# Half a group sooner: moved key sums, projections and key products in an attention kernel with a gated projection behind it

## The chip, the cores and the metric

The kernel runs on one core of one Trainium2 chip. Its metric is the device time of one execution in microseconds (us), the median of several. A second execution is recorded by the hardware profiler; its rows say when each instruction of each engine began and how long it took. The engines are TensorE (PE, with its weight loads as PEld), VectorE (DVE), ScalarE (ACT), GpSimd (POOL), and SyncE (SP), which only issues transfers.

## What is computed

```python
kv_pool = kv.reshape(B, H // 4, 4, W // 4, 4, C).mean(axis=(2, 4))
k = v = kv_pool.reshape(B, -1, C) @ w_sr          # 768 keys of 128 for each of 4 batches
s = (q @ k.transpose(0, 2, 1)) / sqrt(C)          # q: 4 x 12288 x 128
a = exp(s - s.max(-1));  a /= a.sum(-1) + 1e-9
x = a @ v
gate = sigmoid(causal depthwise convolution of x over 5 rows, weights conv_w)
out = (gate * (x @ w_val)) @ w_out
```

All inputs and the output are fp32.

## The kernel before

The 12288 queries of a batch are 24 groups of 512 (`GQ`), 96 groups in all (`G`), and a group is four steps of 128 queries (`NT`). One Python loop over steps `t` writes the order of all engines out by hand: the schedule is manual, so every engine runs its instructions in the order in which the lines of the loop issue them. `j` is the step within the current group; `gi, mj` are group and step lagging by one, and the work of older groups is hung on `mj`.

A step's own work: `score` (L381) makes 128 x 768 scores in PSUM in three passes (queries and keys in a high and a low part), always two steps' worth in the steps with odd `j`. There are three pairs of banks for them. `row_max` (L397, DVE), `expo` (L414, ACT), `norm` (L423, reciprocal of the sum on DVE, with the sum scaled by ACT where `scaled_by_act` says so, else by DVE), `p_hi` (L445, ACT: the fp16 high part `hl`) and `p_lo` (L448, DVE: the remainder, after which the bank is free for the score three steps on). `p_lo` of a group's last step issues the transposing transfer `turn` (L438, SP).

The older groups' work, before the change: the value products of group gi-2 (`av_slice`, L465, PE, in all four steps); x of group gi-3 is written by ACT at mj 0 (`g_x`, L476); the convolution runs on POOL for two groups at a time (`conv_step`, L498: five tap products L491 and four adds L496, spread over eight steps; the last add completes the gate at mj 2 of an odd gi); group gi-6 has its value projection at mj 2 (`g_val`, L549, two fp32 halves; `g_val_parts`, L544, three passes where `split_x`, L537, has made a high and a low part of x on POOL, one group in four), its tanh at mj 2 and the gated product h at mj 3 (`g_h`, L553, DVE); group gi-7 has its output projection at mj 0 (`g_out`, L560) and its evacuation at mj 1 (`g_evac`, L570, ACT). Projections and key products share one PSUM bank, `m` (`misc`, L59), so each has to wait for the user before it. ACT makes the high part of the queries of group gi+2 at mj 3 (`g_qh`, L353) and POOL the low part (`g_ql`, L358).

The next batch's keys are made meanwhile: `plan` (L293) gives places (group, step) to the sums over 4 x 4 pixels (`pool_kv`, L127, DVE), and from these the groups of key products (`setup_product`, L320, at mj 1), column maxima (`column_max`, L196), the scale (`column_scale`, L202), and the high and low parts of the keys (`keys_high`, L235, ACT; `keys_low`, L239, POOL). At each batch boundary `values_parts` (L274) splits the values on POOL in three groups. The last batch, from group 72 on, has no keys to prepare. Output is stored four groups at a time; `held` keeps a store back until the next four are ready, until `CATCH_UP`.

After the loop the last groups (n7 = 89 to n1 = 95) are finished by a list of calls (L820 to L887).

Of the kernel before, what the change touches and what calls it, by code (L numbers as in the profile page):

```python
# [27 lines left out]
def attn_moe_kernel(ctx, tc, qT, kvT, w_sr, w_moe, outT):  # L28
# [264 lines left out]
    def plan():  # L293

        for b in range(1, B):
            st, k0 = states[b], (b - 1) * NG
            if b == 1:
                places = [(k, j) for k in range(4, 21) for j in range(2)] + [(9, 2), (14, 2)]
                loads.update({1: (b, 5), 5: (b, 6), 13: (b, 7)})
                works = [(i, 0, PC) for i in range(WHOLE)]  # L300
            else:
                places = [(-3, 2)] + [(k, j) for k in range(-2, 21) for j in range(2)] + [(-2, 2)]
                early = (-7, -3, -1, 3, 5, 9, 11, 15)
                loads.update({k0 + k: (b, p) for p, k in enumerate(early)})
                works = []
# [7 lines left out]
            for q in range(4):  # L313
                last = max(p for p, w in zip(places, works) if w[0] < (q + 1) * PIECES // 4)
                k = k0 + last[0] + 1
                products[k], highs[k + 1] = (b, q), (b, q)
                maxima[k] = b, q
            scales[k0 + 22] = b
# [8 lines left out]
    def setup_vector(gi, j):  # L327
# [3 lines left out]
        if (gi, j) in sums:  # L331
            b, w = sums[gi, j]
            pool_kv(states[b], *w)
        if j == 2 and gi in maxima:
            b, q = maxima[gi]
            column_max(states[b], q)
        if gi in scales:
            st = states[scales[gi]]
            if j == 0:
                st["scale"] = column_scale(st)  # L340
            for _ in range((3, 2, 1)[j]):
                st["scale"].pop(0)()
# [68 lines left out]
    def scaled_by_act(g, j):  # L411
        return j == 1 or j > 1 and g.i < 9 - j

# [122 lines left out]

    def split_x(g):  # L537
        g.xh, g.xl = (work.tile([C, GQ], F32R, name=n, bufs=1) for n in ("xh", "xl"))
        x = g.x[:, HALO:HALO + GQ]
        nc.gpsimd.tensor_copy(out=g.xh, in_=x)  # L540
        return lambda: nc.gpsimd.tensor_tensor(out=g.xl, in0=x, in1=g.xh.bitcast(F32),
                                               op=ALU.subtract)

# [152 lines left out]
    evac = None  # L696
    held, CATCH_UP, low = [], (B - 1) * NG + 9, None
    for t in range(NT * G + LAG):
# [3 lines left out]
        gi, mj = divmod(t - LAG, NT)  # L702
        avg, xg, vg, og = (at(gi - d) for d in (2, 3, 6, 7))
        cg = at(gi - 4 - gi % 2)

        def projections(c0, c1):
            if og and mj == 0:
                g_out(og.h, og.m, c0, c1)
            if vg and mj == 2:
                if vg.xh is None:  # L710
                    g_val(vg, vg.m, c0, c1)
                elif c0 == 0:
                    g_val_parts(vg, vg.m)

        if og and mj == 0:
            og.m = misc()
        if vg and mj == 2:
            vg.m = misc()
# [15 lines left out]
        if xg and mj == 0:  # L734
            new_x(xg)
            g_x(xg, xg.av)
        if og and mj == 1:
            out_tile(og)
            g_evac(og, og.m)
        evac = None  # L740
        if vg and mj == 2:
            vg.th = g_tanh(vg.gate)
        if gi == 1 and mj > 0:
            evac = values(st, mj - 1)
        elif mj == 1 and gi > 0:
            evac = setup_product(gi)
        if avg:
            av_slice(avg, AV_CUTS[mj], AV_CUTS[mj + 1])
        if cg:
            if mj == 0 and cg.i == gi - 4:  # L750
                halo(cg, at(cg.i - 2), nc.gpsimd)
            conv_step(cg, gi % 2 * 4 + mj)
        if mj == 2 and gi > 7 and gi % 4 == 1:
            low = split_x(at(gi - 5))
        if mj == 3 and gi >= 0 and at(gi + 2):
            g_qh(at(gi + 2))
# [10 lines left out]
        if mj == 1 and gi in highs:  # L767
            b, q = highs[gi]
            keys_high(states[b], q)
        if vg and mj == 3:  # L770
            vg.h = g_h(vg.th, vg.m)
        if gi >= 0 and mj < 3:
            setup_vector(gi, mj)
        if mj == 1 and gi in loads:
            b, p = loads[gi]
# [6 lines left out]
        if mj == 3 and gi in highs:  # L782
            b, q = highs[gi]
            keys_low(states[b], q)
        if mj == 3 and low:
            low()
            low = None
        if mj == 3 and 0 < (gi + 2) // NG < B and (gi + 2) % NG < 3:
# [5 lines left out]
        if mj == 3 and gi >= 0 and at(gi + 2):  # L794
            g_ql(at(gi + 2))
        if og and mj == 2 and og.i % 4 == 3:
            held.append(og)
            if gi > CATCH_UP or len(held) > 1:
                store_last(held.pop(0), 4)
        if gi == CATCH_UP and mj == 2:  # L800
            store_last(held.pop(0), 4)
# [15 lines left out]
    def av_bank():  # L817
        return ps_av.tile([C, GQ], F32, name="av")

    new_x(n3)  # L820
    g_x(n3, n3.av)
    a0, a1 = two()
    n6.m, n5.m = g_val(n6, a0), g_val(n5, a1)
    av_slice(n2, 0, 18)
# [3 lines left out]
    conv_first(n4, acc4)  # L828
    n7.m = g_out(n7.h, misc())
    gate3 = conv_pool(n3)  # L830
# [7 lines left out]
    conv_first(n2, acc2)  # L838
    out_tile(n7)
    g_evac(n7, n7.m)  # L840
    store_last(n7, 2)
# [12 lines left out]
    g_x(n1, avs[0], 0, half)  # L854
    n4.m = g_val(n4, one())
    acc1 = one()
# [3 lines left out]
    n3.m = g_val(n3, av_bank())  # L860
    n4.h = g_h(n4.th, n4.m)
    g_x(n1, avs[1], half, GQ)
    conv_first(n1, acc1[:, half:], half, GQ)
    conv_rest(n1, acc1[:, half:], half, GQ)
# [51 lines left out]
```

## Time and profile before

| | us |
|---|---|
| median of 3 runs | 988.25 (988.19 to 988.72) |
| the profiled execution | 987.91 |
| its span in the trace | 986.1 |

Times of rows are from the span's start. A row of the chain of waits reads: start, length, engine, output tile, line, count. A row of the timeline reads: start, length, engine, line, operation, out<-in, shape, count, and in brackets the idle time ahead of it with what ended it. Matmuls overlap in a row of the timeline; in the chain their lengths add up. Stretches give busy time of each engine and, in brackets, its instructions.

### The profile page before, as it was taken

The numbers are of one execution on the slowest core, as the hardware profiler recorded it, in microseconds if no ns is written. First come the engines' busy times: TensorE is split into PE (matmuls) and PEld (weight loads), VectorE is DVE, ScalarE is ACT, GpSimd is POOL, SyncE is SP. The second block draws the span as 40 slices with busy tenths as digits, with TensorE's granted clock in tenths as the row PEclk, the third lists the DMA queues.
The fourth block names the chain that finished last, engine by engine and source line by source line (L and its number), as shares of the span: only waits on it lengthen the run. The fifth ranks groups of instructions, "written<-read, shape, count | busy, mean of one in ns | idle before, by whom it ended". The sixth has DMA issues, their size and how long they took to land.

```text
span 986.1 us, 14838 instructions
## 1 busy us (share of the span) xinstructions
PE 957.4 (97%) x4837; PEld 718.3 (73%) x4837; DVE 923.1 (94%) x1736; ACT 914.0 (93%) x1698; POOL 908.9 (92%) x700
## 2 busy tenths in 40 slices
PE   4699999999999999999999999999999999999998
PEld 3467777777777777777777777777777777777774
DVE  6999999999999999999999999999999999999996
ACT  2999999999999999999999999999999999999995
POOL 2769999999999999999999999999999999999993
PEclk9999999999999999999999999999999999999999
DMA  9999999999999999999999999999999999999996
GB/s 346 276 220 219 206 163 262 213 244 222 262 238 248 235 257 237 241 249 239 237 241 237 257 229 242 259 229 221 210 221 231 211 217 266 229 195 216 195 213 156
DMA packets 615070, 228.97 MB, mean 232 GB/s; under 512 B 599248, under 2 KB 600400, under 8 KB 609232
## 3 DMA queue, kind: packets, MB, share of 16 engines
q1 hardware_dynamic: 614992, 228.02, 108.4%
q8 instruction: 38, 0.62, 0.3%
q14 instruction: 40, 0.33, 0.1%
HBM read 50.66 MB, written 25.17 MB: 77 GB/s over the span
## 4 chain that ended last, share of the span: by engine, by line
PE 84%; DVE 6%; ACT 5%; POOL 4%; DMA 1%; issue 1%; SPq 0%; POOLq 0%; ACTq 0%; DVEq 0%
PE s L374 35%; PE av L462 33%; PE m L561 7%; PE m L550 6%; ACT hl L446 2%; DVE hl L450 2%; POOL acc L496 2%; ACT s L415 1%; PE m L546 1%; DVE nm L399 1%; DMA pt<-in_kv 1%; POOL tap L491 1%; POOL ql L361 1%; DVE pool L128 0%; DVE s L517 0%
## 5 line engine op out<-in xcount | busy, mean ns | idle before, releaser
L496 POOL TENSOR_TENSOR acc<-acc,tap 128x1024 f32<-128x1024 f32 x184 | 437.0, 2375 | 7.2
L462 PE MATMUL av<-pt,vv 128*128 128x512 f16 x1728 | 404.3, 378 | 0.0
L450 DVE SCALAR_TENSOR_TENSOR hl<-s,r,hl 128x768 f16<-128x768 f32 x384 | 388.4, 1011 | 12.6 <-ACT hl L446 9.0
L399 DVE TENSOR_REDUCE nm<-s 128x1 f32<-128x768 f32 x382 | 361.6, 947 | 17.1 <-PE s L374 6.5
L446 ACT ACTIVATE hl<-s,r 128x768 f16<-128x768 f32 x384 | 346.0, 901 | 16.2 <-DVE r L431 5.0
L415 ACT ACTIVATE s<-s,nm 128x768 f32<-128x768 f32 x384 | 335.7, 874 | 20.3 <-DVE nm L399 14.3
L462 PEld LDWEIGHTS <-vv 128*128 128x128 f16 x1746 | 167.8, 98 | 184.6 <-issue 6.1
L374 PE MATMUL s<-kh,qh 128*128 128x384 f32 x764 | 260.2, 422 | 10.1 <-DVE hl L450 8.3
L491 POOL TENSOR_SCALAR tap<-x,wm 128x1024 f32<-128x1024 f32 x184 | 203.9, 1121 | 0.0
L374 PE MATMUL s<-kh,ql 128*128 128x384 f32 x764 | 195.9, 338 | 0.1
L374 PE MATMUL s<-kl,qh 128*128 128x384 f32 x764 | 195.4, 337 | 0.0
L374 PEld LDWEIGHTS s<-kh,qh 128*128 128x128 f32 x764 | 143.0, 190 | 53.6 <-PE s L374 9.0
L361 POOL TENSOR_TENSOR ql<-q,qh 128x512 fp32r<-128x512 f32 (+1 forms) x97 | 123.2, 1271 | 17.8 <-ACT qh L356 17.8
L374 PEld LDWEIGHTS s<-kh,ql 128*128 128x128 f32 x764 | 138.1, 189 | 0.8 <-POOL ql L361 0.4
L374 PEld LDWEIGHTS s<-kl,qh 128*128 128x128 f32 x764 | 138.5, 188 | 0.0
L561 PE MATMUL m<-h,wm 128*128 128x256 f32 x358 | 106.6, 379 | 0.0
L550 PE MATMUL m<-x,wm 128*128 128x256 f32 x274 | 81.5, 379 | 0.0
L431 DVE RECIPROCAL r<-z 128x1 f32<-128x1 f32 x384 | 61.8, 161 | 10.3
L477 ACT ACTIVATE x<-av,down 128x512 f32<-128x512 f32 x96 | 65.3, 680 | 5.0 <-PE av L462 5.0
L491 POOL TENSOR_SCALAR acc<-x,wm 128x1024 f32<-128x1024 f32 x46 | 51.5, 1120 | 14.8 <-ACT x L477 11.6
L561 PEld LDWEIGHTS m<-h,wm 128*128 128x128 f32 x358 | 64.5, 188 | 0.2
L556 DVE SCALAR_TENSOR_TENSOR h<-th,m 128x512 f32<-128x512 f32 x90 | 60.9, 677 | 0.0
(124 smaller groups left out, 654.9 us busy)
## 6 DMA issues: line engine op xcount, KB each, us to landing
q<-in_q SPq DMA_DIRECT2D x23, 1024.0 KB, 6.0
out<-o SPq DMA_DIRECT2D x22, 1024.0 KB, 4.8
kvt<-in_kv SPq DMA_DIRECT2D x21, 768.0 KB, 5.3
pt<-in_kv SPq DMA_DIRECT2D x12, 384.0 KB, 6.7
o<-in_kv SPq DMA_DIRECT2D x3, 768.0 KB, 9.5
pt<-hl SPq DMA_TRANSPOSE x98, 10.3
out<-o SPq DMA_DIRECT2D x3, 512.0 KB, 2.7
kvt<-in_kv SPq DMA_DIRECT2D x2, 384.0 KB, 7.3
```

Source lines behind the costliest of these rows:

```text
L361: nc.gpsimd.tensor_tensor(out=g.ql[:, c0:c1], in0=g.q[:, c0:c1], in1=g.qh[:, c0:c1].bitcast(F32), op=ALU.subtract)
L374: nc.tensor.matmul(g.s[j][:, h], a[:, sl], k[:, h * HALF:(h + 1) * HALF], start=(i == 0), stop=(i == 2))
L399: nc.vector.tensor_reduce(out=nm, in_=g.s[j], axis=AX.XY, op=ALU.max, negate=True)
L415: nc.scalar.activation(out=g.s[j], in_=g.s[j], func=AF.Exp, bias=g.nm.pop(j), accum_out=g.z[j])
L446: nc.scalar.activation(out=part(g, j, 0), in_=g.s[j], func=AF.Copy, scale=g.r[j])
L450: nc.vector.scalar_tensor_tensor(out=part(g, j, 1), in0=g.s.pop(j), scalar=g.r.pop(j), in1=part(g, j, 0), op0=ALU.mult, op1=ALU.subtract)
L462: nc.tensor.matmul(out, g.st["vv"][:, v, k], g.pt[:, j0:j1, a * NCH + k], start=(i == 0), stop=(i == len(AV_ORDER) - 1))
L477: nc.scalar.activation(out=g.x[:, HALO + c0:HALO + c1], in_=av, func=AF.Copy, scale=g.st["down"])
L491: nc.gpsimd.tensor_scalar(out=t, in0=g.two[:, k:k + 2 * GQ], scalar1=cwt[:, k:k + 1], scalar2=1.0, op0=ALU.mult, op1=ALU.mult)
L496: nc.gpsimd.tensor_tensor(out=g.acc, in0=g.acc, in1=t, op=ALU.add)
L550: nc.tensor.matmul(m[:, c0:c1], wval, g.x[:, HALO + c0:HALO + c1], start=True, stop=True)
L561: nc.tensor.matmul(m[:, c0:c1], wout, h[:, c0:c1], start=True, stop=True)
```

## The change

- The key sums go to steps 0 and 3 in place of 0 and 1; the places (-3, 2) and (-2, 2) of batches 2 and 3 become (5, 2) and (12, 2). The key products are issued at mj 3, the column maxima a group later at step 0, the operations of the scale at steps 1, 2 and 3.
- The value projection of group gi-6 moves to mj 0, tanh and h to mj 1, the output projection (now of the same group gi-6) to mj 2, its evacuation to mj 3. `CATCH_UP` becomes group 79 and the stores follow at mj 3. The high part of the queries moves to mj 2.
- POOL's two operations that split x stand together at mj 0 of every fourth group, ahead of that group's two adds, and no longer at mj 2 and 3 behind them.
- In the last batch (`QUIET`) one more group in four is projected in parts: ACT writes xh at mj 1, DVE xl at mj 2 (groups 70, 74, 78, 82, 86, 90); for groups 91 and 92 ACT writes xh and POOL xl, in the tiles of the queries.
- `scaled_by_act` changes: steps 0 and 2 of groups 1 to 5 besides step 1 of all groups.
- Behind the loop, n7 is finished but for its store; n6, n5 and n4 are projected in parts; h of n4 is made by POOL (two operations) and ACT (a copy out of PSUM), not by DVE.

```diff
@@ -295,11 +295,11 @@
         for b in range(1, B):
...
             if b == 1:
-                places = [(k, j) for k in range(4, 21) for j in range(2)] + [(9, 2), (14, 2)]
+                places = [(k, j) for k in range(4, 21) for j in (0, 3)] + [(9, 2), (14, 2)]
                 loads.update({1: (b, 5), 5: (b, 6), 13: (b, 7)})
...
             else:
-                places = [(-3, 2)] + [(k, j) for k in range(-2, 21) for j in range(2)] + [(-2, 2)]
+                places = [(k, j) for k in range(-2, 21) for j in (0, 3)] + [(5, 2), (12, 2)]
                 early = (-7, -3, -1, 3, 5, 9, 11, 15)
...
                 works = []
@@ -314,7 +314,7 @@
                 last = max(p for p, w in zip(places, works) if w[0] < (q + 1) * PIECES // 4)
...
                 products[k], highs[k + 1] = (b, q), (b, q)
-                maxima[k] = b, q
+                maxima[k + 1] = b, q
             scales[k0 + 22] = b
...
     def setup_product(gi):
@@ -331,14 +331,14 @@
         if (gi, j) in sums:
...
             pool_kv(states[b], *w)
-        if j == 2 and gi in maxima:
+        if j == 0 and gi in maxima:
             b, q = maxima[gi]
...
             st = states[scales[gi]]
-            if j == 0:
+            if j == 1:
                 st["scale"] = column_scale(st)
-            for _ in range((3, 2, 1)[j]):
+            for _ in range((0, 3, 2, 1)[j]):
                 st["scale"].pop(0)()
...
     def quad_tile(g):
@@ -409,7 +409,7 @@
             nc.vector.tensor_reduce(out=g.nm[j], in_=g.nm2[j], axis=AX.X, op=ALU.min)
...
     def scaled_by_act(g, j):
-        return j == 1 or j > 1 and g.i < 9 - j
+        return j == 1 or j % 2 == 0 and 0 < g.i < 6
 
...
         nc.scalar.activation(out=g.s[j], in_=g.s[j], func=AF.Exp, bias=g.nm.pop(j),
@@ -534,12 +534,13 @@
         nc.scalar.activation(out=th, in_=gate, func=AF.Tanh, scale=0.5)
...
 
-    def split_x(g):
-        g.xh, g.xl = (work.tile([C, GQ], F32R, name=n, bufs=1) for n in ("xh", "xl"))
-        x = g.x[:, HALO:HALO + GQ]
-        nc.gpsimd.tensor_copy(out=g.xh, in_=x)
-        return lambda: nc.gpsimd.tensor_tensor(out=g.xl, in0=x, in1=g.xh.bitcast(F32),
-                                               op=ALU.subtract)
+    def part_high(g, copy, names=("xh", "xl"), bufs=1):
+        g.xh, g.xl = (work.tile([C, GQ], F32R, name=n, bufs=bufs) for n in names)
+        copy(out=g.xh, in_=g.x[:, HALO:HALO + GQ])
+
+    def part_low(g, eng):
+        eng.tensor_tensor(out=g.xl, in0=g.x[:, HALO:HALO + GQ], in1=g.xh.bitcast(F32),
+                          op=ALU.subtract)
 
...
         for i, (w, x) in enumerate(((wvh, g.xh), (wvl, g.xh), (wvh, g.xl))):
@@ -694,27 +695,25 @@
         row_max_half(at(0), j, 1)
...
     evac = None
-    held, CATCH_UP, low = [], (B - 1) * NG + 9, None
+    held, CATCH_UP, QUIET = [], (B - 1) * NG + 7, (B - 1) * NG
     for t in range(NT * G + LAG):
...
         gi, mj = divmod(t - LAG, NT)
-        avg, xg, vg, og = (at(gi - d) for d in (2, 3, 6, 7))
+        avg, xg, vg = (at(gi - d) for d in (2, 3, 6))
         cg = at(gi - 4 - gi % 2)
...
         def projections(c0, c1):
-            if og and mj == 0:
-                g_out(og.h, og.m, c0, c1)
             if vg and mj == 2:
+                g_out(vg.h, vg.m, c0, c1)
+            if vg and mj == 0:
                 if vg.xh is None:
...
 
-        if og and mj == 0:
-            og.m = misc()
-        if vg and mj == 2:
+        if vg and mj % 2 == 0:
             vg.m = misc()
...
             score(nxt, (j + 1) % NT)
@@ -734,15 +733,15 @@
         if xg and mj == 0:
...
             g_x(xg, xg.av)
-        if og and mj == 1:
-            out_tile(og)
-            g_evac(og, og.m)
+        if vg and mj == 3:
+            out_tile(vg)
+            g_evac(vg, vg.m)
         evac = None
-        if vg and mj == 2:
+        if vg and mj == 1:
             vg.th = g_tanh(vg.gate)
...
             evac = values(st, mj - 1)
-        elif mj == 1 and gi > 0:
+        elif mj == 3 and gi > 0:
             evac = setup_product(gi)
...
             av_slice(avg, AV_CUTS[mj], AV_CUTS[mj + 1])
@@ -750,9 +749,17 @@
             if mj == 0 and cg.i == gi - 4:
...
             conv_step(cg, gi % 2 * 4 + mj)
-        if mj == 2 and gi > 7 and gi % 4 == 1:
-            low = split_x(at(gi - 5))
-        if mj == 3 and gi >= 0 and at(gi + 2):
+        by_pool = at(gi - 5) if gi > 7 and gi % 4 == 1 else None
+        by_others = at(gi - 5) if gi > QUIET and gi % 4 == 3 else None
+        by_both = at(gi - 3) if G > gi >= G - 2 else None
+        if by_pool and mj == 0:
+            part_high(by_pool, nc.gpsimd.tensor_copy)
+            part_low(by_pool, nc.gpsimd)
+        if by_others and mj == 1:
+            part_high(by_others, nc.scalar.copy)
+        if by_both and mj == 2:
+            part_high(by_both, nc.scalar.copy, ("qh", "ql"), 2)
+        if mj == 2 and gi >= 0 and at(gi + 2):
             g_qh(at(gi + 2))
...
             g_qh(at(1))
@@ -767,10 +774,12 @@
         if mj == 1 and gi in highs:
...
             keys_high(states[b], q)
-        if vg and mj == 3:
+        if vg and mj == 1:
             vg.h = g_h(vg.th, vg.m)
-        if gi >= 0 and mj < 3:
+        if gi >= 0:
             setup_vector(gi, mj)
+        if by_others and mj == 2:
+            part_low(by_others, nc.vector)
         if mj == 1 and gi in loads:
...
             load_kv(b, states[b], 2 * p)
@@ -782,9 +791,8 @@
         if mj == 3 and gi in highs:
...
             keys_low(states[b], q)
-        if mj == 3 and low:
-            low()
-            low = None
+        if mj == 3 and by_both:
+            part_low(by_both, nc.gpsimd)
         if mj == 3 and 0 < (gi + 2) // NG < B and (gi + 2) % NG < 3:
...
         if mj == 0 and 0 < gi // NG < B and gi % NG == 1:
@@ -793,11 +801,11 @@
         drip(convert, 1 if t else 2)
...
             g_ql(at(gi + 2))
-        if og and mj == 2 and og.i % 4 == 3:
-            held.append(og)
+        if vg and mj == 3 and vg.i % 4 == 3:
+            held.append(vg)
             if gi > CATCH_UP or len(held) > 1:
                 store_last(held.pop(0), 4)
-        if gi == CATCH_UP and mj == 2:
+        if gi == CATCH_UP and mj == 3:
             store_last(held.pop(0), 4)
...
     n1, n2, n3, n4, n5, n6, n7 = groups[:-8:-1]
@@ -817,16 +825,18 @@
     def av_bank():
...
 
+    def val(g, m):
+        return g_val_parts(g, m) if g.xh is not None else g_val(g, m)
+
     new_x(n3)
...
     a0, a1 = two()
-    n6.m, n5.m = g_val(n6, a0), g_val(n5, a1)
+    n6.m, n5.m = val(n6, a0), val(n5, a1)
     av_slice(n2, 0, 18)
...
     conv_first(n4, acc4)
-    n7.m = g_out(n7.h, misc())
     gate3 = conv_pool(n3)
...
     n5.h = g_h(n5.th, n5.m, h=spare.pop())
@@ -836,8 +846,6 @@
     halo(n2, n4, nc.scalar)
...
     conv_first(n2, acc2)
-    out_tile(n7)
-    g_evac(n7, n7.m)
     store_last(n7, 2)
...
     conv_rest(n2, acc2)
@@ -852,14 +860,18 @@
     g_evac(n5, n5.m)
...
     g_x(n1, avs[0], 0, half)
-    n4.m = g_val(n4, one())
+    n4.m = val(n4, one())
     acc1 = one()
...
     n3.m = g_val(n3, av_bank())
-    n4.h = g_h(n4.th, n4.m)
+    n4.h = work.tile([C, GQ], F32, name="h", bufs=1)
+    nc.gpsimd.tensor_scalar(out=n4.th, in0=n4.th, scalar1=1.0, scalar2=1.0,
+                            op0=ALU.add, op1=ALU.mult)
     g_x(n1, avs[1], half, GQ)
+    nc.scalar.copy(out=n4.h, in_=n4.m)
+    nc.gpsimd.tensor_tensor(out=n4.h, in0=n4.th, in1=n4.h, op=ALU.mult)
     conv_first(n1, acc1[:, half:], half, GQ)
...
```

## Rows read from the trace of the kernel before

**Rows 1.** The page, first part: busy us, share of the span, instructions.

```profile
PE 957.4 (97%) x4837; PEld 718.3 (73%) x4837; DVE 923.1 (94%) x1736; ACT 914.0 (93%) x1698; POOL 908.9 (92%) x700
```

**Rows 2.** Stretches: length, then busy us of PE, PEld, DVE, ACT, POOL; clock; DMA.

```profile
64.50:82.70 18.20, 17.23 (x85) 11.56 (x85) 17.27 (x32) 17.09 (x35) 17.45 (x12) 1.00 1.10 230
...
800.00:900.00 100.00, 100.00 (x512) 75.96 (x511) 91.96 (x167) 95.33 (x175) 96.57 (x69) 1.00 1.08 227
```

**Rows 3.** Waits of PE from 90 to 970 us: total us, times, longest.

```profile
PE s L374 <- DVE r L431: 0.6, 2, 0.3
```

**Rows 4.** The chain of waits, 600 to 640 us: start, length, what.

```profile
628.37 0.43 PE m L550 x2
...
630.27 1.94 PE av L462 x9
...
638.16 0.69 PE m L546 x3
```

**Rows 5.** Timeline of POOL, 236 to 285 us.

```profile
275.71 4.82 POOL L496 TENSOR_TENSOR acc<-acc,tap 128x1024 f32<-128x1024 f32 x2
280.48 0.60 POOL L540 CAST xh<-x 128x512 fp32r<-128x512 f32 x1
281.16 1.27 POOL L541 TENSOR_TENSOR xl<-x,xh 128x512 fp32r<-128x512 f32 x1
```

**Rows 6.** Timeline of ACT, 278 to 285 us.

```profile
281.32 0.60 ACT L571 ACTIVATE o<-m 128x512 f32<-128x512 f32 x1
```

**Rows 7.** Timelines of POOL and ACT at the two later boundaries.

```profile
516.62 0.61 POOL L540 CAST xh<-x 128x512 fp32r<-128x512 f32 x1
...
517.44 0.60 ACT L571 ACTIVATE o<-m 128x512 f32<-128x512 f32 x1
...
752.47 0.61 POOL L540 CAST xh<-x 128x512 fp32r<-128x512 f32 x1
...
753.06 0.60 ACT L571 ACTIVATE o<-m 128x512 f32<-128x512 f32 x1
```

**Rows 8.** Timelines of ACT, DVE and PE, 842 to 850 us.

```profile
845.91 0.62 ACT L356 CAST qh<-q 128x512 fp32r<-128x512 f32 x1
846.47 0.90 ACT L446 ACTIVATE hl<-s,r 128x768 f16<-128x768 f32 x1
...
847.16 0.68 DVE L556 SCALAR_TENSOR_TENSOR h<-th,m 128x512 f32<-128x512 f32 x1
847.75 1.01 DVE L450 SCALAR_TENSOR_TENSOR hl<-s,r,hl 128x768 f16<-128x768 f32 x1
...
849.00 0.70 PE L374 MATMUL s<-kh,qh 128*128 128x384 f32 x2
```

**Rows 9.** Timelines of DVE and POOL, 33 to 35 us, and line 249's durations.

```profile
33.55 0.42 DVE L100 TENSOR_TENSOR tap<-tap 128x261 int32<-128x261 int32 x1
...
33.74 0.58 POOL L249 TENSOR_SCALAR vt<-vt,up 128x256 f32<-128x256 f32 x1 [0.43 <-DVE up L224]
...
L249 POOL TENSOR_SCALAR vt<-vt,up x12: 474/478/582, 33.7 to 742.6; 128x256 f32<-128x256 f32 x12
```

**Rows 10.** Timelines of POOL and DVE in the last batch, two places.

```profile
842.37 4.82 POOL L496 TENSOR_TENSOR acc<-acc,tap 128x1024 f32<-128x1024 f32 x2
...
844.07 0.96 DVE L399 TENSOR_REDUCE nm<-s 128x1 f32<-128x768 f32 x1 [0.26 <-PE s L374]
...
919.44 4.81 POOL L496 TENSOR_TENSOR acc<-acc,tap 128x1024 f32<-128x1024 f32 x2
...
922.09 0.96 DVE L399 TENSOR_REDUCE nm<-s 128x1 f32<-128x768 f32 x1 [0.27 <-PE s L374]
```

**Rows 11.** The chain of waits and the timelines of DVE and ACT behind the loop.

```profile
968.43 0.86 PE m L561 x2
...
976.00 0.68 DVE L556 SCALAR_TENSOR_TENSOR h<-th,s 128x512 f32<-128x512 f32 x1
...
976.18 0.48 ACT L513 ACTIVATE s<-x,wm 128x256 f32<-128x256 f32 x1 [0.74 <-DVE s L517]
```

## The prediction

> **What bounds the kernel now.** I read the page's busy shares first: four engines stand at 92 to 97% of the span [rows 1]. That leaves two questions, which engine paces the loop and how far behind it the others are. The stretches answer the first: from 800 to 900 us TensorE (PE) is busy 100.00 us of 100, VectorE (DVE) 91.96, ScalarE (ACT) 95.33, GpSimd (POOL) 96.57; before 82.7 us PE still idles 0.97 us in 18.2, over four pairs of steps [rows 2]. Between 90 and 970 us PE waits 0.6 us in all [rows 3]. So the loop is a row of matmuls without a hole, and its chain names prices: half a projection in fp32 0.43 us, nine value products 1.94 us, a whole projection in three parts 0.69 us [rows 4]. Only less PE work, a wait that newly reaches PE, or the two ends can move the time.
>
> How near are such waits? A step is: row maximum (DVE), exponential, scaled copy hl (ACT), remainder hl (DVE), which frees a bank for a later score. In the step with qh, ACT ends hl at 847.37, DVE begins the remainder at 847.75, because the gated product h stands ahead of it, and ends at 848.76; PE uses the bank at 849.00 [rows 8]. ACT may thus be late by 0.38 + 0.24, about 0.6 us, DVE by 0.24, or by some 0.6 where no h stands ahead.
>
> All sums are made against the profiled execution, 987.91 us (span 986.1 and 1.8 around it). The median of the runs is 988.25, so 0.34 is added at the end.
>
> **Value projections in parts.** ACT now makes high parts for groups 70, 74, 78, 82, 86, 90, and DVE their low parts; ACT and POOL do groups 91 and 92. Each saves PE 2 x 0.43 - 0.69 = 0.17 us [rows 4]. Five of them are projected in the loop, in the last batch where PE never waits: -0.86. The ACT copy (0.62, as the qh cast [rows 8]) goes in ahead of hl and uses up that step's 0.6 us; between 0 and 0.1 us each, taken as 0.
>
> **The low part on DVE** is the term that I think decides. It subtracts xh from x, 128x512 fp32, both in SBUF, behind the row maximum of the third step. Its own time: the h product, same size, holds DVE 0.59 us to the next start (847.16 to 847.75 [rows 8]); that much the slack of 0.6 us covers. But in the loop DVE does no operation today that reads two SBUF tiles: h and hl take one of theirs from PSUM. In the start-up there is one such operation: 33.55 to 33.97 on DVE, and the POOL instruction that began at 33.74 inside it took 0.58 us, the longest of twelve whose median is 0.478 and least 0.474 [rows 9]. Taken at its face, the two engines kept each other out. POOL is the one that is nearly always at work, so in the loop DVE would be the one to wait. Where will POOL be? At 845.03 the row maximum ends; POOL's two adds run from 842.37 to 847.19, the second from about 844.8: 2.2 us to wait. Two quads later DVE is ready at 923.05 and the add ends at 924.25: 1.2 us [rows 10]. There are five such places in the loop before its last group; by the same two engines' rows at each the wait would be 0.4, 1.2, 2.2, 1.2, 1.2 us, mean 1.2. DVE is then late by the wait plus 0.59, the next 1/sum and with it hl as well, 0.6 is absorbed, and PE stands for about the wait. Bounds: 0 (no exclusion) to 5 x 2.4 (a whole add each); I take 1.1 x 5 = +5.5, since PE's stops let POOL get ahead. Queued behind the waiting DVE: remainder and reciprocal of the next step, then ACT's hl, then PE's scores.
>
> The Trainium skill (SBUF — State Buffer, section "SBUF: two separate sides") states that DVE and GpSimd share a port pair, and that a DVE operation with two SBUF inputs and a GpSimd operation reading SBUF exclude each other for the whole instruction. The start-up row agrees in kind, with 0.10 us; no row here shows DVE as the one that waits. By that rule the sum is the forecast below, without it 989.0.
>
> **Tanh a step sooner, POOL's split earlier.** Value projection, tanh, h, output projection and evacuation move by two steps, tanh by one, since h now follows it in the same step. The swap is nearly symmetric for PE, DVE and ACT: h takes the place in front of the remainder that a key sum had, and the key sum goes to where h was. PSUM bank m keeps its order of three users. Not symmetric is POOL. Tanh needs the gate, whose last add POOL ends near 280.53; behind it today come xh and xl [rows 5]. The change puts both ahead of the two adds, in every fourth group, so the gate comes (281.16 + 1.27) - 280.53 = 1.9 us later, at 282.4. And tanh now stands where the evacuation starts today, 281.32 [rows 6]: 1.1 us too early. Most groups have 2 to 5 us there and absorb it; just behind a batch boundary, where POOL has split the values besides, they don't. The other two boundaries: add done 516.6, slot 517.44, so 1.1 us short; 752.5 and 753.06, so 1.3 us [rows 7]. ACT is in order: hl, the next exponential and qh queue behind the waiting tanh, DVE behind hl, PE behind DVE. With 0.6 us absorbed each, PE loses 0.5 + 0.5 + 0.7, some 1.8; bounds 0 and the whole 3.5; I take +2.0.
>
> **Key sums, maxima, key products, qh.** The same 36 or 48 sums, in steps 0 and 3 instead of 0 and 1; the column maxima a group later, the scale operations (some 0.15 us each) a step later, beside h. PE's only two waits in the loop, 0.3 us each [rows 3], may vanish or be doubled: 0 with bounds -0.6 and +0.6. The key products keep their place behind an evacuation, one pair of steps on. SP's queue keeps its order of transposes; the stores come behind the transpose of the group before, and the key loads do not move: 0. Qh a step sooner frees POOL from waits that lie before 65 us, where ACT paces: 0.
>
> **The start.** Projections begin half a group sooner, so one more output projection (2 x 0.43) falls into the loop; it meets a pair of steps in which PE idles 0.97/4 = 0.24 [rows 2]: +0.6, bounds 0 and 0.86.
>
> **The tail.** Output projection n7 leaves it (0.86, in the chain at 968.43 [rows 11]), and n6 and n5 come in parts (2 x 0.17): PE reaches the last value products 1.2 us sooner. h of n4 leaves DVE, where it sat at 976.00 between the two halves of the last convolution, but the second half had to wait for ACT anyway: conv_first only begins at 976.18 [rows 11]. So this move itself gains nothing, and ACT's new copy of n4.m stands right ahead of that conv_first and takes some 0.2 back. Sum -1.0, bounds -0.6 and -1.2.
>
> **Sum:** -0.86 + 5.5 + 2.0 + 0.6 - 1.0 = +6.2; 987.91 + 6.2 + 0.34 = 994.5 us.
>
> **The rivals.**
> A, the forecast, both waits reach PE: 994.5 (993.5 to 997.5). Chance 0.46.
> B, DVE waits for POOL, but tanh does not (POOL running at least 1.3 us less behind at the boundaries than today): 994.5 - 2.0 = 992.5. For it, that an early POOL absorbs all other gates; against it three rows that agree to 0.2 us. 0.12.
> C, no exclusion between DVE and POOL: the subtract costs 0.59 and is hidden. 994.5 - 5.5 = 989.0, up to 990.5 if each tanh costs its whole wait. For it: one start-up row of 0.10 us is little, and it has POOL as the one kept out. 0.24.
> D, not slower: neither wait reaches PE, so that only PE's saved work and the tail count. 994.5 - 5.5 - 2.0 = 987.0; with a start that costs nothing and a tail worth 1.2, 986.2. It decides from slack: if hl may be late by 1.3 us, not 0.6, without PE noticing. Against it: rows 8. 0.12.
> E, the change makes a heavier wait: every DVE subtract meets a whole add (2.4 us) and each tanh costs its full wait, 994.5 + 6.5 + 1.5 = 1002.5, or a part of this. 0.06.
>
> **How the numbers follow.** A measurement of this kernel tells about 0.2%, 2 us, from no change: 986.3 and 990.2. Faster: half of D, 0.06. Same: the other half of D and three quarters of C, 0.06 + 0.18 = 0.24. Slower: A, B, E and a quarter of C, 0.46 + 0.12 + 0.06 + 0.06 = 0.70. The range reaches from C's low end, 988.4, to A's high end, 997.5, and leaves out D and E, 0.18.
>
> **What would show it.** The low part on DVE: its mean is near 0.6 us in C and D, well over 1.2 in A and B, and PE waits for hl or 1/sum once in each of five quads after 765 us. The tanh: ACT waits for POOL's acc near 282, 518 and 755 us, 1 us or more, and PE stops just behind. PE's busy time must fall by about 1.4 us (eight times 0.17). The chain after the loop's end must be about 1 us shorter. Wrong it would be if PE's waits between 90 and 970 us stay under 2 us.

## The result and the profile after

| | before | after |
|---|---|---|
| median of 4 runs, us | 988.32 (988.19 to 988.72) | 1000.81 (1000.26 to 1000.87) |
| the profiled execution | 987.91 | 1000.87 |
| its span | 986.1 | 999.1 |

The changed kernel takes 1.0124 times as long (95% interval 1.0107 to 1.0142), 12.5 us more by the medians, 13.0 us by the two spans. The page of after and its stretch from 800 to 900 us answer to [rows 1, 2]:

```profile
PE 964.4 (97%) x4837; PEld 716.1 (72%) x4837; DVE 930.4 (93%) x1744; ACT 906.2 (91%) x1704; POOL 916.5 (92%) x704
```

```profile
800.00:900.00 100.00, 97.82 (x488) 71.40 (x486) 93.34 (x161) 90.91 (x170) 91.50 (x63) 1.00 1.03 216
```

PE has less work than before, yet its busy time rose from 957.4 to 964.4 us. The count in the stretch is the better witness: 488 matmuls in 100 us where there were 512. The waits of after from 90 to 975 us (total, times, longest) name the cause only in part, first PE's, to be held against [rows 3], then three of ACT's:

```profile
PE s L374 <- DVE z L429: 5.1, 14, 0.8
PE s L374 <- DVE hl L450: 2.0, 7, 0.3
```

```profile
ACT hl L446 <- DVE r L431: 31.2, 82, 0.7
ACT hl L446 <- issue: 9.6, 5, 2.3
ACT th L534 <- POOL acc L496: 3.3, 3, 1.3
```

These rows give 7.1 us for PE; before they gave 0.6. A waiting matmul is partly counted as busy, so I also worked out every stop from the starts alone: the time from one score's second pass to the next, less the usual time (the median) of the same matmuls. By starts PE stops for 15.8 us from 90 to 970 us, and for 2.3 us before. In what follows a "stop" is this figure, good to some 0.03 us. ACT's waits for DVE's 1/sum (the second fence's first row) were 1.6 us before; yet shift_alone below has 33.2 us of them and hardly a stop, so they are what a schedule with another order looks like, not the cause. The second row is another matter: its five waits, for which the profile names no releaser, are 2.3 us once and 1.8 us four times, and one stands behind each of the five low parts on DVE in the loop.

Where the time comes in is told by the start of the exponential of step 0 of a group, after less before:

| group | 6 | 13 | 37 | 61 | 74 | 77 | 81 | 85 | 89 | 93 | 95 |
|---|---|---|---|---|---|---|---|---|---|---|---|
| us | 0.34 | 1.40 | 2.88 | 4.35 | 4.83 | 7.68 | 9.26 | 10.87 | 12.43 | 14.03 | 13.83 |

Up to group 74 each batch costs about 1.5 us. From there every fourth group adds some 1.6 us, the first 2.85 (the last boundary's wait for the gate falls in there too). Line 542 is the one that makes low parts (columns: least, median and longest duration in ns, first and last start):

```profile
L542 POOL TENSOR_TENSOR xl<-x,xh x22: 1267/1282/1302, 115.8 to 953.6; 128x512 fp32r<-128x512 f32 x22
L542 DVE TENSOR_TENSOR xl<-x,xh x6: 674/2123/2622, 772.4 to 975.1; 128x512 fp32r<-128x512 f32 x6
```

On DVE it takes 0.67 us once, at 975.08, where it begins between two of POOL's adds; the other five take 2.1 to 2.6 us. One such group in the timeline of after, 810 to 825 us, all engines:

```profile
810.27 4.83 POOL L496 TENSOR_TENSOR acc<-acc,tap 128x1024 f32<-128x1024 f32 x2
...
813.54 2.12 DVE L542 TENSOR_TENSOR xl<-x,xh 128x512 fp32r<-128x512 f32 x1
...
814.27 2.10 PE L462 MATMUL av<-pt,vv 128*128 128x512 f16 x9
...
815.06 1.71 POOL L361 TENSOR_TENSOR ql<-q,qh 128x512 fp32r<-128x512 f32 x1
...
815.58 1.00 DVE L450 SCALAR_TENSOR_TENSOR hl<-s,r,hl 128x768 f16<-128x768 f32 x1
...
816.63 0.62 PE L374 MATMUL s<-kh,qh 128*128 128x384 f32 x2 [0.26 <-DVE z L429]
...
816.93 0.90 ACT L446 ACTIVATE hl<-s,r 128x768 f16<-128x768 f32 x1 [1.82 <-issue]
...
817.09 0.51 PE L374 MATMUL s<-kl,qh 128*128 128x384 f32 x2
...
818.93 0.62 PE L374 MATMUL s<-kh,qh 128*128 128x384 f32 x2 [0.29 <-DVE hl L450]
...
820.09 2.12 PE L462 MATMUL av<-pt,vv 128*128 128x512 f16 x9
...
822.40 0.51 PE L374 MATMUL s<-kl,qh 128*128 128x384 f32 x2
...
824.08 0.59 PE L374 MATMUL s<-kh,qh 128*128 128x384 f32 x2 [0.32 <-DVE z L429]
```

DVE's subtract begins at 813.54, while POOL is in its two adds, and ends at 815.66, some 0.6 us after they do at 815.10. POOL's next operation, ql, began at 815.06 inside the subtract's last stretch and took 1.71 us, where it takes 1.28 elsewhere. So each held the other up: DVE stood for 2.12 - 0.67 = 1.45 us, then POOL for 0.43. The remainder hl begins 2.04 us behind the subtract (813.54 to 815.58). ACT's hl, which it needs, ended at 813.76, so the remainder is 1.8 us late; ACT's next hl, behind DVE's 1/sum, is late by as much (816.93), and PE pays three times: from nine value products to the second pass of the next score it usually needs 2.31 us (820.09 to 822.40), here 2.82 (814.27 to 817.09); then comes 0.57 at the score of 818.93 and 0.63 at that of 824.08. The lateness goes on through the row of DVE and ACT, step by step, until three scores have taken a part each.

### The profile page after: what moved, and what is told of

It is laid out like the page before. It is cut to its first block, busy times and chain, and to the rows that moved or that the text cites. A ratio compares the mean times of both kernels' runs of the same rounds, so it can differ in the third digit from the quotient of the medians.

```text
span 999.1 us, 14962 instructions
## 1 busy us (share of the span) xinstructions
PE 964.4 (97%) x4837; PEld 716.1 (72%) x4837; DVE 930.4 (93%) x1744; ACT 906.2 (91%) x1704; POOL 916.5 (92%) x704
## 4 chain that ended last, share of the span: by engine, by line
PE 61%; ACT 14%; DVE 12%; POOL 9%; issue 2%; DMA 1%; SPq 0%; ACTq 0%; POOLq 0%; DVEq 0%
PE s L374 25%; PE av L462 24%; ACT hl L446 7%; DVE hl L450 6%; PE m L562 5%; POOL acc L496 4%; PE m L551 4%; ACT s L415 4%; DVE nm L399 2%; POOL tap L491 2%; ACT x L477 1%; DVE h L557 1%; POOL ql L361 1%; PE m L547 1%; DVE r L431 1%
## 5 line engine op out<-in xcount | busy, mean ns | idle before, releaser
L374 PEld LDWEIGHTS s<-kh,qh 128*128 128x128 f32 x764 | 140.8, 190 | 68.5 <-DVE hl L450 15.0
L361 POOL TENSOR_TENSOR ql<-q,qh 128x512 fp32r<-128x512 f32 (+1 forms) x97 | 125.4, 1293 | 13.6 <-ACT qh L356 13.5
L551 PE MATMUL m<-x,wm 128*128 128x256 f32 (+1 forms) x254 | 75.7, 379 | 0.0
```

Source lines behind the costliest of these rows:

```text
L361: nc.gpsimd.tensor_tensor(out=g.ql[:, c0:c1], in0=g.q[:, c0:c1], in1=g.qh[:, c0:c1].bitcast(F32), op=ALU.subtract)
L374: nc.tensor.matmul(g.s[j][:, h], a[:, sl], k[:, h * HALF:(h + 1) * HALF], start=(i == 0), stop=(i == 2))
L551: nc.tensor.matmul(m[:, c0:c1], wval, g.x[:, HALO + c0:HALO + c1], start=True, stop=True)
```

## The experiments

**Theory.** The low part on DVE and POOL's operations on SBUF exclude each other, DVE waits, and PE stands for most of it; tanh's wait behind POOL's split costs some 2 us more. **Rivals.** DVE is simply too full for 0.67 us more; PE loses for another reason in the last batch (the copy on ACT, the projections' new places); or the loss lies in the move by half a group itself.

**low_pool** gives the low part to POOL.

```diff
-            part_low(by_others, nc.vector)
+            part_low(by_others, nc.gpsimd)
```

> The changed kernel (1000.8 us) with one edit: the low part of x for groups 70 to 90 is subtracted by GpSimd, not by VectorE, at the same place. The changed trace has six such VectorE subtracts of 1.96 us in the mean and PE stops of 9.2 us just behind five of them. Theory 1 (VectorE waits for the GpSimd instruction that is running): these stops go, about 992 us, less what GpSimd's added 1.3 us per four groups may cost where it delays a gate (0 to 1 us). Rival (what PE waits for in this stretch is ScalarE's added copy ahead of hl, or the projection's new place): at least half of the 9.2 us stays, 996 us or more.

Measured: 996.33 us (1.0083, 1.0068 to 1.0098), in the rival's range by its time, though the waits name another reason: 8.0 us over the kernel before, which took 988.30 beside it, where after is 12.5 over. Such excesses, each against the runs of before on the same chip, are compared from here on. PE's waits, 90 to 975 us, and the one stop that is left in the last batch:

```profile
PE s L547 <- POOL xl L542: 2.1, 1, 2.1
...
PE m L547 <- POOL xl L542: 1.5, 1, 1.5
```

```profile
776.24 0.39 PE L547 MATMUL m<-xh,wvh 128*128 128x512 f32 x1
776.47 0.40 PE L547 MATMUL m<-xh,wvl 128*128 128x512 f32 x1
778.36 0.50 PE L547 MATMUL m<-xl,wvh 128*128 128x512 f32 x1 [1.50 <-POOL xl L542]
```

The other four groups have no stop left. Instead PE waits once for POOL's xl, 1.8 us, because POOL, still behind from the batch boundary, comes to it only at 777.05; and behind the loop it waits 2.1 us, where POOL now has a low part more among its work. With the 4.1 us that no_others below is over, these two make the 8.0; the 0.7 us that the parts save is offset by a longer stop at 285 us (1.03 for 0.57) and by the start-up's scatter. The copy on ACT, which is still there, costs no stop. So the stops behind DVE's part go with it, and POOL's part brings waits of its own; shift_pool_low below has neither.

**low_psum** replaces the subtract by an operation of DVE of the same size that takes one input from PSUM. It writes zeros, so the low part of x is left out.

```diff
-            part_low(by_others, nc.vector)
+            nc.vector.scalar_tensor_tensor(out=by_others.xl, in0=by_others.xh.bitcast(F32),
+                scalar=0.0, in1=vg.m, op0=ALU.mult, op1=ALU.mult)
```

> The changed kernel with the VectorE subtract replaced by a VectorE operation of the same size that takes one input from SBUF (xh) and one from PSUM (the output projection) and writes zeros as the low part: it leaves out the low part of x in those groups. Theory 1 (two SBUF inputs against a running GpSimd instruction): the operation takes about 0.7 us, as h does, PE stops less than 2 us in the stretch, 992 to 993 us. Rival (0.6 us more of VectorE's time in this step are enough): the operation takes 0.7 us too, but the time stays at 998 us or more.

Measured: 997.97 us (1.0097, 1.0081 to 1.0114), not the 992 to 993 of the theory. Line 782 is the new operation; the second fence is DVE's wait for it:

```profile
L782 DVE SCALAR_TENSOR_TENSOR xl<-xh,m x6: 686/687/689, 773.3 to 972.7; 128x512 fp32r<-128x512 f32 x6
```

```profile
DVE xl L782 <- PE m L562: 5.0, 5, 1.3
```

The operation takes 0.69 us in all six cases, beside POOL's adds or the ql that follows them. But the PSUM tile that it reads is the output projection that PE is still writing, and DVE stood 1.0 us in each of the five groups for that. The edit put a new wait in place of the old one: for the duration it speaks clearly, for the time of the kernel it decides nothing.

**b_two512, b_two64 and b_one512** put one more operation of DVE into the kernel before, six times in the last batch, with a result that nobody uses: two SBUF inputs of 512 columns, two of 64, and one of 512.

```diff
+        if mj == 2 and gi > (B - 1) * NG and gi % 4 == 3:
+            g = at(gi - 5)
+            nc.vector.tensor_tensor(out=work.tile([C, GQ], F32R, name="xl", bufs=1)[:, :512],
+                in0=g.x[:, HALO:HALO + 512], in1=g.x[:, :512], op=ALU.subtract)
```

b_two64 has 64 in the place of each 512 there. b_one512 has in the same place:

```diff
+            nc.vector.tensor_reduce(out=small.tile([C, 1], F32, name="big", bufs=2),
+                in_=at(gi - 5).x[:, HALO:HALO + GQ], axis=AX.X, op=ALU.max)
```

> The kernel before (988.3 us) with one VectorE operation of 128x512 added at the third step of groups 75, 79, 83, 87, 91 and 95, both inputs in SBUF, its result unused. Theory 1: its mean is 1.5 to 2.5 us and the time rises by 4 to 8 us, to 992 to 996. Rival (0.6 us of load): mean 0.6 us, time within 1 us of before.

> As b_two512, but on 64 columns of the 512, an eighth of the work. Theory 1: the wait for the running GpSimd add stays, the mean is 0.8 to 2 us, and the time rises by 1 to 5 us. Rival (load): the mean is about 0.15 us and the time is that of before.

> The kernel before with one VectorE operation of 128x512 added at the place of b_two512, but with a single input, in SBUF: a maximum over x whose result is unused. It measures the load alone: about 0.6 us each, as GpSimd cannot be in its way if two inputs are what matters. Theory 1 (exclusion needs two SBUF inputs): mean 0.5 to 0.7 us, time at most 1 us above before, where b_two512 gave +6.8. Rival (any VectorE operation that reads SBUF there is delayed by GpSimd): mean over 1.2 us and +4 or more.

Measured: 995.06 us (1.0068, 1.0053 to 1.0083), 992.64 (1.0045, 1.0030 to 1.0060) and 988.76 (1.0009, 1.0000 to 1.0019, beside 987.96). The operation's own row in each, in that order, durations in ns:

```profile
L776 DVE TENSOR_TENSOR xl<-x x6: 1081/2094/2153, 767.5 to 967.9; 128x512 fp32r<-128x512 f32 x6
```

```profile
L776 DVE TENSOR_TENSOR xl<-x x6: 610/1645/1699, 767.2 to 965.3; 128x64 fp32r<-128x64 f32 x6
```

```profile
L775 DVE TENSOR_REDUCE big<-x x6: 667/674/675, 766.9 to 961.5; 128x1 f32<-128x512 f32 x6
```

This parts the theory from "DVE is too full". Six operations that each occupy DVE for 0.67 us cost 0.8 us in all; six of about the same work with two SBUF inputs cost 6.8 us. An eighth of the columns still takes 1.43 us in the mean, against 1.88: what is paid is the wait, not the work. And the wait has a sharp end: each of the six operations of b_two64 ends 0.07 to 0.09 us behind the POOL instruction that was running when it began, as here, where POOL's two adds end at 847.63 and DVE's operation at 847.72:

```profile
842.79 4.84 POOL L496 TENSOR_TENSOR acc<-acc,tap 128x1024 f32<-128x1024 f32 x2
```

```profile
846.04 1.68 DVE L776 TENSOR_TENSOR xl<-x 128x64 fp32r<-128x64 f32 x1
```

b_one512 writes one column only, but the operation of low_psum writes 512 with one input in SBUF and isn't held up either, so it is the second SBUF input that counts. The load itself isn't quite free in the new order, which has less slack (below): of 0.6 us some 0.3 would reach PE, 1.5 us for five subtracts. That is an estimate; no run has the load alone there.

**no_others** is after without the additional groups in parts in the last batch.

```diff
-        by_others = at(gi - 5) if gi > QUIET and gi % 4 == 3 else None
+        by_others = at(gi - 5) if gi > G else None
```

> The changed kernel without the further projections in parts of groups 70 to 90: no ScalarE copy and no VectorE subtract, these six projections are in fp32 again. Theory 1: the 9.2 us of PE stops go and 5 x 0.17 of PE work come back, 1000.8 - 9.2 + 0.9 = 992.5. Rival (the projections' new places cost in the last batch too): 995 or more.

Measured: 992.09 us (1.0042, 1.0027 to 1.0057), 4.1 over, so 8.4 less than after. All that PE still waits for from 90 to 975 us is one row:

```profile
PE s L374 <- DVE z L429: 2.2, 6, 0.5
```

By starts, six stops over 0.3 us are left, all at batch boundaries: at 247, 484 and 722 us (0.79, 0.79, 0.46), and at 287, 524 and 761 us (0.58, 0.51, 0.83). The next three kernels are about these.

**no_split_at_bounds** is after without POOL's split in the one group behind each boundary (20, 44, 68; these are projected in fp32).

```diff
-        by_pool = at(gi - 5) if gi > 7 and gi % 4 == 1 else None
+        by_pool = at(gi - 5) if gi > 7 and gi % 4 == 1 and gi % NG != 1 else None
```

> The changed kernel, but GpSimd's split of x is left out for groups 20, 44 and 68, whose projections are in fp32. The gate of these groups is then complete 1.9 us sooner. Theory (tanh waits for the gate there; the PE stops behind it sum to 2.3 us in the changed trace): these stops go, three projections cost 0.17 more, -1.7 us, about 999.1. Rival (the tanh's wait of about 1.1 us is hidden, the stops come from VectorE): no change or +0.5.

Measured: 997.69 us (1.0098, 1.0083 to 1.0113), 9.7 over, so 2.8 less than after. The three waits of tanh for the gate, 3.3 us in after, are down to

```profile
ACT th L534 <- POOL acc L496: 0.3, 1, 0.3
```

and the stops at 287, 525 and 762 us are gone. These were 2.3 us and three projections in parts go with them (+0.4), so some 1.9 was to be had. The rest is an interaction: the first group with a subtract on DVE, at 776 us, comes 14 us behind the last of these stops, POOL stands elsewhere there, the subtract takes 1.37 us and not 2.62, and the group's stops are 1.26 us less, just about the same.

**scale_late** puts the three scale operations of step 1 of after into step 2, away from h.

```diff
-            if j == 1:
+            if j == 2:
                 st["scale"] = column_scale(st)
-            for _ in range((0, 3, 2, 1)[j]):
+            for _ in range((0, 0, 5, 1)[j]):
```

> The changed kernel with the scale's operations at steps 2 and 3 (five and one) and none at step 1, where h stands. In the changed trace PE stops 0.78, 0.80 and 0.46 us just behind step 1 of groups 22, 46 and 70. Theory (three small operations behind h delay the remainder): these stops fall by at least half, -1 to -2 us, 999 to 1000. Rival (VectorE is late there anyhow from the maxima and sums of step 0): less than 0.5 us.

Measured: 1000.58 us (1.0126, 1.0110 to 1.0141 beside 987.96), 12.6 over: the 1 to 2 us that were expected do not show, though the interval leaves room for a part of them. Yet the stops behind the scale fell as meant, 0.78 to 0.34, 0.80 to 0.34, 0.46 to none. About half of it came back some 40 us later, where the stops at 285, 524 and 761 us became 1.22, 0.76 and 0.99. ACT's wait for the gate at the first boundary, in after and then in scale_late:

```profile
284.00 0.63 ACT L534 ACTIVATE th<-acc 128x512 f32<-128x512 f32 x1 [1.06 <-POOL acc L496]
```

```profile
283.08 0.63 ACT L534 ACTIVATE th<-acc 128x512 f32<-128x512 f32 x1 [1.21 <-POOL acc L496]
```

ACT waits a little longer for POOL there, by 0.15, 0.15 and 0.05 us at the three boundaries, and the two later stops grew by about as much. A likely reason is that a stop of PE ahead of a boundary gives the late POOL time; that is not tested. The first stop has another cause: PE waits for the next batch's values to land.

```profile
282.68 2.12 PE L462 MATMUL av<-pt,vv 128*128 128x512 f16 x9 [1.05 <-DMA vv<-hv]
```

Their transfer left SP's queue only at 278.79, behind a transposing transfer that held the queue for 11.11 us there and 8.98 in after. low_pool, with the scale where after has it, shows the same wait (0.88 us, behind a transfer of 10.94), so moving the scale need not be its cause.

**shift_alone** joins the last three edits: the move by half a group, without the subtract on DVE, without the splits at the boundaries, with the scale a step on.

> The changed kernel with three parts undone at once: no further projections in parts for groups 70 to 90, no split of x at groups 20, 44 and 68, scale operations at steps 2 and 3. What is left is the move by half a group, the key sums, maxima and products, and the tail. If the three causes add: 992.1 (without the further projections) - 1.4 (the three gate waits, less three projections) - 1.0 (the scale) = about 989.7; before is 988.0 to 988.3. If the move itself costs more than one output projection (0.86), 991 or more; if it gains, below 987.5.

Measured: 989.67 us (1.0018, 1.0009 to 1.0027), 1.5 over, so 2.6 less than no_others. Of stops over 0.3 us only 0.36 and 0.35 are left, behind the scale. The move by half a group itself, with the tail and the three projections that are back in fp32 (0.4), is worth about +1.5 us, not the 12.5: the third rival falls.

**shift_pool_low** adds to shift_alone the projections in parts of four groups of the last batch, high part by ACT and low part by POOL.

```diff
-        by_others = at(gi - 5) if gi > G else None
+        by_others = at(gi - 5) if G - 1 > gi > QUIET + 6 and gi % 4 == 3 else None
...
-            part_low(by_others, nc.vector)
+            part_low(by_others, nc.gpsimd)
```

**b_pool_low** does the same in the kernel before and nothing else.

```diff
+        quiet = (B - 1) * NG + 6 < gi < G - 1 and gi % 4 == 3
+        if quiet and mj == 1:
+            more = at(gi - 5)
+            more.xh, more.xl = (work.tile([C, GQ], F32R, name=n, bufs=1) for n in ("xh", "xl"))
+            nc.scalar.copy(out=more.xh, in_=more.x[:, HALO:HALO + GQ])
...
+        if quiet and mj == 3:
+            nc.gpsimd.tensor_tensor(out=more.xl, in0=more.x[:, HALO:HALO + GQ],
+                                    in1=more.xh.bitcast(F32), op=ALU.subtract)
```

> shift_alone, with four projections in parts put back (groups 74, 78, 82 and 86), ScalarE making the high and GpSimd the low part. Theory 1 (the gain of parts was real and only VectorE's two-input operation ate it): 4 x 0.17 = 0.7 us below shift_alone, no new PE stop in the last batch. Rival (ScalarE's copy ahead of hl costs too): not below shift_alone, PE stops behind each copy.

> The kernel before with four more projections in parts (groups 74, 78, 82 and 86), ScalarE making the high and GpSimd the low part. Theory 1: 0.7 us below before, 987.3 to 987.6, if GpSimd's 1.3 us more per four groups still leave every gate early. Rival (the copy ahead of hl, or a late gate, reaches PE): equal to before or slower.

Measured: 989.00 us (1.0010, 1.0001 to 1.0019), 0.67 less than shift_alone, near 4 x 0.17, though the two intervals overlap; and 987.06 us (0.9991, 0.9982 to 1.0000), 1.1 less than before. The traces are finer. From group 77 to 95 the start of the exponential gains 0.56 us on before in shift_pool_low and 0.53 in b_pool_low (the other 0.5 of b_pool_low's gain is there by group 6, ahead of the edit), while shift_alone gains none: 0.13 to 0.14 us for each projection in parts. The lines of b_pool_low: the low parts on POOL, then PE's only wait from 90 to 975 us, the same as in [rows 3]:

```profile
L791 POOL TENSOR_TENSOR xl<-x,xh x4: 1274/1279/1296, 809.1 to 925.3; 128x512 fp32r<-128x512 f32 x4
```

```profile
PE s L374 <- DVE r L431: 0.6, 2, 0.3
```

The projections in parts gain, if a little less than the 0.17 us that the chain names, and ACT's copy costs nothing; what spoilt them was the engine that made the low part. b_pool_low is the fastest kernel of the study, though its interval ends at 1.

**b_split_first** puts, in the kernel before, POOL's two split operations ahead of the adds, as the change does, with tanh left where it was.

```diff
-        if mj == 2 and gi > 7 and gi % 4 == 1:
-            low = split_x(at(gi - 5))
+        if mj == 0 and gi > 7 and gi % 4 == 1:
+            split_x(at(gi - 5))()
```

> The kernel before with GpSimd's split of x ahead of the two adds, as in the change, and all else as it was. Its tanh is a step later than in the changed kernel, and the gates at groups 20, 44 and 68 come 3.1, 3.1 and 2.7 us ahead of it in the trace of before, so 1.9 us later they are still in time. Theory (only the early split and the early tanh together make the wait): no change, within 0.5 us of before, and no wait of ScalarE for acc. Rival (the split's place alone costs): 1 us or more.

Measured: 988.19 us (1.0003, 0.9994 to 1.0012), and ACT never waits for the gate. The early split by itself costs nothing; it is the tanh a step sooner that meets it.

## Why the prediction was right and wrong

The direction, the mechanisms and their places held; the size did not: 994.5 us was forecast, 1000.81 measured. The terms, against the 13.0 us between the spans:

| term, us | forecast | found |
|---|---|---|
| projections in parts | -0.86 | -0.7 (0.14 each, as in shift_pool_low) |
| low part on DVE | +5.5 | +9.2 |
| tanh and POOL's split | +2.0 | +2.3 |
| key sums, maxima, scale | 0 | +0.9 |
| start | +0.6 | up to +0.86 |
| tail | -1.0 | -0.8 |
| not assigned | | about 1.2 |

**The low part on DVE** is the term that was mis-sized. That DVE would be the one to wait, and why, was right; the row of 0.10 us in the start-up [rows 9] was a true sign. By the page of the Trainium skill that the prediction weighed (SBUF — State Buffer, section "SBUF: two separate sides") whoever starts first keeps the other out for the whole instruction; this trace agrees both ways, with DVE's 1.45 us behind the adds and POOL's 0.43 us behind the subtract. Two of its numbers failed. First, the wait: from [rows 10] and three more such places I took 1.2 us in the mean, then 1.1, "since PE's stops let POOL get ahead". Measured are 1.95 us in the first group and 1.45 in each of the other four, mean 1.55: a likely reason, not tested, is that a stop does not let POOL get ahead when POOL is itself held up by the same subtract (its two adds took 5.14 us at 772.15, against 4.82 in [rows 10]). That is 5 x 0.45 = 2.2 us. Second, the step "0.6 is absorbed": the remainder began 2.55 us behind the subtract in the first group and about 2.05 in the others, together 10.7, and PE stopped for 9.2, so 0.3 was absorbed in each group. Nearly all of this lies ahead of the remainder, where DVE would have waited for ACT's hl in any case: in shift_pool_low the same remainder begins 1.11 us behind its row maximum (808.57 to 809.68), in after 2.90 (812.68 to 815.58), so it is 1.8 us late, and PE stands for 1.7. Behind it there is next to no slack. [rows 8] show how late hl may be in one step; here all that follows in the row of DVE and ACT is late too, and three scores feel it. That is 5 x 0.3 = 1.5 us. In the kernel before, from which the 0.6 was read, 0.44 to 0.48 us is absorbed behind each operation of b_two512 in the loop: the reading was somewhat high there too, and the new order has less. Rival E held the heavier wait of the two ("every DVE subtract meets a whole add") and came nearest, though its way of getting there, with 2.4 us at each, is not what happened.

**Tanh** was sized nearly right, with some luck. ACT's waits, 1.06, 0.96 and 1.29 us, are those that were forecast; the stops just behind are 0.71, 0.61 and 0.94 us, 2.3 in all for 2.0, so here too 0.35 was absorbed each time and not 0.6, and the rounding of 1.8 up to 2.0 made up for a part of that. no_split_at_bounds and b_split_first show both halves of the cause. POOL in the timeline of after, to be held against [rows 5]: the split now stands ahead of the adds, which end at 283.96.

```profile
277.21 0.61 POOL L539 CAST xh<-x 128x512 fp32r<-128x512 f32 x1
277.90 1.27 POOL L542 TENSOR_TENSOR xl<-x,xh 128x512 fp32r<-128x512 f32 x1
279.13 4.83 POOL L496 TENSOR_TENSOR acc<-acc,tap 128x1024 f32<-128x1024 f32 x2
```

**The scale** was put down at 0, bounds -0.6 and +0.6. It is +0.9: stops of 0.78, 0.80 and 0.46 us against 0.56 and 0.56 in the like places before. The timeline of DVE in after, around the first:

```profile
244.72 0.68 DVE L557 SCALAR_TENSOR_TENSOR h<-th,m 128x512 f32<-128x512 f32 x1
245.31 0.15 DVE L220 TENSOR_REDUCE big<-parts 128x1 f32<-128x4 f32 x1
245.50 0.15 DVE L221 TENSOR_SCALAR pw<-big 128x1 int32<-128x1 int32 x1
245.69 0.15 DVE L223 TENSOR_SCALAR pw<-pw 128x1 f32<-128x1 f32 x1
245.76 1.01 DVE L450 SCALAR_TENSOR_TENSOR hl<-s,r,hl 128x768 f16<-128x768 f32 x1
```

The prediction named this ("beside h") and left it unpriced. h and the three operations hold the remainder up by 1.04 us (244.72 to 245.76), where before they stood in different steps; the slack of [rows 8] was already spent on h.

**Start and tail.** Between groups 6 and 13 after loses 1.06 us, so the output projection that came into the loop was not hidden by PE's idle 0.24 us; its upper bound, 0.86, is the likelier. The tail gave 0.8 for 1.0 (13.83 us at group 95, 13.0 at the end). The chain of waits behind the loop shows what took the rest back: ACT's copy of n4.m lies on it with 0.48 us, not 0.2. The sixth subtract held POOL's adds at 972.65 to 5.33 us, but they are not on the chain.

```profile
987.92 0.70 PE s L547 x3
...
988.64 0.48 ACT h L873
...
989.17 0.49 ACT s L513
```

**What was to show it.** The low part's duration, ACT's three waits for the gate and PE's waits behind them came as named; behind each subtract PE stopped three times, not once. That PE's busy time must fall by 1.4 us was a bad sign to name: it rose by 7.0, as a matmul's record can run on while it waits (the wait rows hold 7.1 us of the 15.8 us of stops).

**By runs alone**, without a stop worked out: of the 12.5 us, 8.4 go with the subtract on DVE and the projections that it serves (no_others), 2.6 with the splits at the boundaries and the scale together (shift_alone), and 1.5 are the rest of the move. What stays open: some 1.2 us of the 13.0. 0.34 us of it is there by group 6, ahead of any projection; scale_late and no_split_at_bounds, which are the same kernel up to there, stand at -0.46 and +0.57, so that is the start-up's own scatter. Most of the rest, about 0.5 us in each of the second and third batches, is in stops below 0.3 us. They sum to 2.4 us in after, 0.8 before and 3.1 in shift_alone, so they come with the move, but I could not lay them to one cause.

## What to carry to other kernels

Before an elementwise operation goes to a VectorE with room to spare, look at what GpSimd does in that moment and at where both inputs lie: with two inputs in SBUF beside a busy GpSimd, 0.67 us of work cost 2.1, with one input 0.67. Price a late step not by the slack of one step, least of all one read from the old order, but by how far the lateness runs on in the row of engines that feed each other: here a remainder 1.8 us late cost 1.7. And count stops by the starts of the bounding engine's instructions; its busy share and its wait rows showed less than half of them here.

## What of the hardware was unexpected

The exclusion holds for tiny operations as well: 64 columns on VectorE took 1.65 us (median), and even the least of the six, 0.61, ended just behind the POOL instruction that was running. It costs GpSimd too, 0.43 us on a subtract of 1.28. And an operation held up in this way shows no idle time and no releaser in the trace: it only looks long.
